# The w_out stage of a fused attention and MoE kernel as seven products of quarters per batch, with one set of eight PSUM places

## The chip, the cores and the metric

The kernel runs on one core of a Trainium2 chip. The metric is the time of one execution on the device in microseconds. The median of three runs before the change is 670.9 us, the lowest 670.52 and the highest 672.65.

## The reference

Three blocks follow one another: attention over 4 batches, a first MoE block, and a second one, which alone is changed. With `x` the output of the first block (4 batches of 576 tokens and 512 features):

```python
def _moe2_ref(x, w_in, g_ln, w_sg, b_sg, w_out):
    h = x @ w_in                                   # 512 -> 1024
    h = gelu_tanh(h)
    u, v = (h[..., :512], h[..., 512:])
    v_n = (v - mean(v)) / np.sqrt(var(v) + 1e-06) * g_ln
    v_s = np.einsum('ts,bsd->btd', w_sg, v_n) + b_sg[None, :, None]
    gated = u * v_s
    return (x + gated @ w_out).astype(np.float32)  # w_out: 512 x 512
```

## The kernel before

All work is recorded first and emitted later, so nearly every instruction has the line of the emitter (L664) in the profile; one tells them apart by the names of their tiles. Each large product is made three times over: both operands are kept as a high part (type fp32r) and a low rest, and high times high, high times low and low times high are added up in PSUM (`passes`, L872). Making such a pair costs a copy on ScalarE (`copy`) and a subtraction on VectorE or GpSimd (`sub`); the table `WHO` (L667) says on which engine.

The second MoE block runs batch by batch (b = 0 to 3), each with these stages:

- **V** (`stage_v`, L1608): x times the second half of w_in, token tiles of 128 as rows, 12 matmuls of 512 columns per tile, into PSUM tiles `V`; then gelu on ScalarE, the normalisation on VectorE (`st`, `ag`, `rs`, `vt`), and the pair `vh`, `vl`. Even batches have a fifth tile for the last 64 tokens of two batches.
- **U** (`stage_u`, L1667): x times the first half of w_in, 8 groups of 12 matmuls of 288 columns, into PSUM tiles `M`, then gelu into `U`.
- **S** (`stage_s`, L1682): w_sg times the normalised v, 8 groups of 14 matmuls of 288 columns, into `M`. Behind each group VectorE scales it into `gt`, GpSimd multiplies by `U`, ScalarE copies to `gh`, VectorE subtracts to `gl`.
- **O** (`stage_o`, L1723): w_out times the gated values, for two batches at once: 3 column blocks of 384 by 4 row blocks, each a group of 12 matmuls of 384 columns into PSUM tiles `O`. One VectorE instruction (two where a block spans both batches) adds half of `X2` and writes `o`, which SyncE stores.

The order of the recorded stages is V0 U0 S0, V1 U1 S1, V2 O(0,1) U2 S2, V3 U3 S3, O(2,3). PSUM has three rings of places in this block: 3 for `V`, 3 for `M`, 2 for `O`. `w_out` is loaded as 64-bit words and turned to single precision by five VectorE and two ScalarE instructions of 1024 columns for each half (`w_bits`, `w_pair`), among the work of S0. A list scheduler (`Plan.schedule`) then plays the recorded instructions through a table of durations and fixes each engine's order; within one ring, places are given out in the recorded order.

Of the kernel before, what the change touches and what calls it, by code (L numbers as in the profile page):

```python
# [11 lines left out]
I32 = mybir.dt.int32  # L12
# [314 lines left out]
class Plan:  # L327
# [337 lines left out]


WHO = dict(oN="A", wl="V", wc="V", Q="A", K="A", Ql="P", Kl="P", V="A", Vl="P", PH="A", O="A", xh="A", xl="P", kh="A", kl="P",  # L667
           X="A", Xl="V", vh="V", vl="V", gU="P", gh="A", gl="V", sg="A", sl="V", R2="AV", R="A", P="VA", PL="V", um="A")
ALT = 400.0
MB = 100  # L670
CB = 300
# [35 lines left out]
LD1 = 6  # L707
AHEAD = 3
T1 = 2


def cost(n):
    return n / 2.4 + 13
# [3 lines left out]
def fused_kernel(ctx: ExitStack, tc: tile.TileContext, low, high, tails, mu,  # L717
# [114 lines left out]
    def w_bits(key, vtile):  # L832

        raw = w1[key]
        low, high = raw[:, :, :, 0], raw[:, :, :, 1]
# [735 lines left out]
    def wt3(shape, dt):  # L1571
        return gtile(shape, dt, "w", 2)

    def ut3():
        return gtile([128, 1024], I32, "u", 1).rearrange("p (c n) -> p c n", n=512)

    loads, conv = weight_list(("wout", w_out, 4, (0,), 1.0, wt3, ut3))
# [30 lines left out]
    def stage_v(b):  # L1608
# [73 lines left out]
    def stage_s(b):  # L1682
        vh, vl = VN.pop(b)
        vt = VT.pop(b)
        sh, sl = sg
        if b % 2 == 0:
            GT[b // 2] = gtile([128, 4, 2 * S], F32R, "gh"), gtile([128, 4, 2 * S], F32R, "gl")
        gh, gl = [x[:, :, S * (b % 2):S * (b % 2) + S] for x in GT[b // 2]]
        order.need(("V", b), ("U", b))
        for f in range(2):  # L1690
            fs = slice(f * HF, (f + 1) * HF)
            for m in range(4):
                ms = slice(128 * m, 128 * m + 128)
                p, mk = ptile("M", HF, 3)
                pe(14 * cost(HF))
                for c in range(4):
                    mm(p, vh[:, c, ms], sh[:, c, fs], start=c == 0)
                    mm(p, vh[:, c, ms], sl[:, c, fs])
                    mm(p, vl[:, c, ms], sh[:, c, fs])
                mm(p, vt[:, ms], sh[:, 4, fs])  # L1700
                mm(p, vt[:, ms], sl[:, 4, fs], stop=True)
                gt = gtile([128, HF], F32, "gt", 2)

                def e0(p=p, gt=gt, m=m, fs=fs):
                    nc.vector.scalar_tensor_tensor(out=gt, in0=p, scalar=g_col[:, m:m + 1], in1=b_bc[:, fs],
                                                   op0=ALU.mult, op1=ALU.add)

                def e1(gt=gt, m=m, fs=fs):
                    tt("gU", gt, gt, U[b][:, m, fs], ALU.mult)

                def e2(gt=gt, m=m, fs=fs):
                    copy("gh", gh[:, m, fs], gt)

                def e3(gt=gt, m=m, fs=fs):
                    sub("gl", gl[:, m, fs], gt, gh[:, m, fs].bitcast(F32))

                at(0, e0, mk)
                at(400, e1)
                at(1200, e2)
                at(1700, e3, ("G", b, f))  # L1720
                yield

    def stage_o(p2):  # L1723
        gh, gl = GT.pop(p2)
        W = 2 * S // 3
        for f in range(3):
            fs = slice(W * f, W * f + W)
            spans = [(2 * p2 + x, max(W * f, S * x), min(W * f + W, S * x + S)) for x in range(2) if W * f < S * x + S and S * x < W * f + W]
            order.need(*[("G", b, g) for b, t0, t1 in spans for g in range(2)])
            for m in range(4):  # L1730
# [3 lines left out]
                o = gtile([128, W], F32, "o", 3)  # L1734

                def e0(p=p, o=o, m=m, spans=spans, f=f):
                    for b, t0, t1 in spans:
                        os, xs = slice(t0 - W * f, t1 - W * f), slice(t0 - S * (b % 2), t1 - S * (b % 2))
                        nc.vector.scalar_tensor_tensor(out=o[:, os], in0=X2[b][:, m, xs], scalar=0.5, in1=p[:, os], op0=ALU.mult, op1=ALU.add)
                        nc.sync.dma_start(out=outT[b, 128 * m:128 * m + 128, xs], in_=o[:, os])  # L1740

                at(0, e0, mk)
                yield

    load_tails(0)
    load_x2(0)
    take(loads, 99)
# [3 lines left out]
    raw4, raw1 = gtile([128, 4, 2 * S], F32, "gh")[:, :, 0:S], gtile([128, 4, 2 * S], F32, "gl")[:, 0, 0:S]  # L1751
# [9 lines left out]
    work += conv  # L1761
    for b in range(B):
        for _ in stage_v(b):
            pass
        if b == 2:
            for _ in stage_o(0):
                pass
        for _ in stage_u(b):
            take(work)
        if b + 1 < B:  # L1770
# [3 lines left out]
            XHL[b + 1] = wtile([128, 2, 4, S], F32R, "XHL")  # L1774
            for t in range(5):
                at(1000 + 1500 * t, lambda t=t, b=b: split_x2(b + 1, 128 * t, min(S, 128 * t + 128)), ("xs", b + 1, t))
        for _ in stage_s(b):
            take(work)
    for _ in stage_o(1):
        pass  # L1780
    order.run()
    plan.schedule()
    plan.emit()
    for p in (pcm, gcm, wcm, dram, const):
        p.close()


# [62 lines left out]
```

## Time and profile before

| what | value |
|---|---|
| median of three runs | 670.9 us |
| the profiled execution | 669.56 us, of which 667.5 us are the span of the profile |
| granted TensorE clock over the span | 0.999 |
| TensorE matmuls busy | 659.0 us (99%), 4074 of them |
| VectorE busy | 471.4 us (71%) |
| ScalarE busy | 420.2 us (63%) |
| GpSimd busy | 231.8 us (35%) |
| second MoE block on TensorE | from 453.4 to 664.1 us |

The page gives busy time of each engine, the same in 40 slices, and the chain of work that ended last. The views of the trace used below are the chain in order of time, groups of instructions by form in a stretch, the instructions of one tile, busy time by stretch, and the order of time on one engine. A matmul's listed duration is longer than the distance to the next one, since they are pipelined; the distance is read from the chain.

### The profile page before, as it was taken

What the parts mean: (1) busy time and instruction counts of PE and PEld (TensorE: products, weight loads), DVE (VectorE), ACT (ScalarE), POOL (GpSimd) and SP (SyncE); (2) the same over time, 40 slices, a digit from 0 to 9 for tenths busy, and PEclk for the clock granted to TensorE, in tenths of its full rate; (3) what the DMA queues carried; (4) which work ended last, traced back from release to release, by engine and by line L of the source; (5) the groups of instructions that cost most, each with busy time, mean ns of one, the idle gap of its engine ahead of it and who ended that gap; (6) DMA issues with size and microseconds to landing.
All of it is one profiled execution on the core that took longest, in us unless ns stands there. A gap on an engine that the chain in (4) does not pass through costs nothing.

```text
span 667.5 us, 11918 instructions
## 1 busy us (share of the span) xinstructions
PE 659.0 (99%) x4074; PEld 608.9 (91%) x4074; DVE 471.4 (71%) x1306; ACT 420.2 (63%) x1095; POOL 231.8 (35%) x278
## 2 busy tenths in 40 slices
PE   9999999999999999999999999999999999999997
PEld 8978777889999999999999889998999989998997
DVE  4979999997678888886886766765796574166232
ACT  6998987689867999898888865834433320132210
POOL 3033334146613456565454513601151410041220
PEclk9999999999999999999999999999999999999999
DMA  9894421233224345321233008207700002300012
GB/s 333 308 357 149 162 93 36 99 120 105 67 76 125 98 141 163 114 59 58 98 122 105 26 2 299 72 25 225 275 2 1 1 0 88 127 1 1 1 50 92
DMA packets 35244, 71.36 MB, mean 107 GB/s; under 512 B 6256, under 2 KB 18032, under 8 KB 35184
## 3 DMA queue, kind: packets, MB, share of 16 engines
q1 hardware_dynamic: 35040, 70.60, 31.4%
q8 instruction: 32, 0.52, 0.4%
q14 instruction: 28, 0.23, 0.1%
q10 hardware_dynamic: 144, 0.00, 0.0%
HBM read 59.05 MB, written 9.44 MB: 103 GB/s over the span
## 4 chain that ended last, share of the span: by engine, by line
PE 82%; ACT 7%; DVE 5%; DMA 3%; issue 2%; SPq 1%; POOL 0%; ACTq 0%; DVEq 0%; POOLq 0%
PE M L664 40%; PE O L664 18%; PE S L664 10%; PE T L664 8%; PE V L664 6%; ACT P L664 2%; DMA w<-w_out_dram 1%; DVE wv L664 1%; DMA q<-Q 1%; ACT wv L664 1%; DVE P L664 1%; DVE PL L664 1%; DVE xT L664 1%; SPq L664 1%; DMA kh<-low_dram 0%
## 5 line engine op out<-in xcount | busy, mean ns | idle before, releaser
L664 ACT ACTIVATE PH<-T 128x384 fp32r<-128x384 f32 (+3 forms) x152 | 65.8, 434 | 31.5 <-PE T L664 27.3
L664 DVE TENSOR_TENSOR PL<-T,PH 128x384 fp32r<-128x384 f32 (+1 forms) x128 | 63.4, 504 | 31.4 <-ACT PH L664 20.5
L664 PE MATMUL M<-xh,w 128*128 128x384 f32 (+1 forms) x272 | 75.8, 341 | 0.0
L664 PE MATMUL M<-xh,wv 128*128 128x256 f32 (+2 forms) x264 | 71.6, 359 | 0.0
L664 PE MATMUL M<-kh,wv 128*128 128x320 f32 (+2 forms) x256 | 70.1, 347 | 0.0
L664 PE MATMUL T<-ident,P 128*128 128x128 f32 x320 | 68.7, 277 | 1.3 <-DVE PL L664 0.5
L664 ACT ACTIVATE P<-S,nb 128x128 f32<-128x128 f32 (+2 forms) x124 | 65.7, 538 | 6.4 <-DVE P L664 5.6
L664 DVE TENSOR_SCALAR_CACHE_REDUCE P<-S 128x128 f32<-128x128 f32 (+2 forms) x124 | 58.7, 489 | 15.0 <-PE S L664 8.6
L664 POOL TENSOR_TENSOR gt<-gt,U 128x288 f32<-128x288 f32 x32 | 30.9, 968 | 95.9 <-ACT XHL L664 48.6
L664 POOL TENSOR_TENSOR Q<-qkv,Q 64x256 fp32r<-64x256 f32 x32 | 25.2, 787 | 108.9 <-ACT Q L664 79.6
L664 POOL TENSOR_TENSOR xl<-t,xh 128x384 fp32r<-128x384 f32 (+1 forms) x40 | 39.8, 1002 | 49.6 <-ACT xh L664 47.1
L664 PEld LDWEIGHTS T<-ident,P 128*128 128x128 f32 x320 | 42.2, 141 | 13.6 <-DVE P L664 3.7
L664 POOL TENSOR_TENSOR kl<-R,kh 128x384 fp32r<-128x384 f32 (+1 forms) x40 | 41.1, 1031 | 37.0 <-ACT kh L664 36.9
L664 PE MATMUL M<-XHL,w 128*128 128x288 f32 x384 | 51.7, 294 | 0.0
L664 PEld LDWEIGHTS M<-XHL,w 128*128 128x128 f32 x384 | 51.4, 188 | 0.2
L664 PE MATMUL O<-gh,w 128*128 128x384 f32 x192 | 49.6, 337 | 0.0
L664 PEld LDWEIGHTS M<-xh,w 128*128 128x128 f32 x272 | 48.1, 189 | 1.4
L664 PEld LDWEIGHTS M<-xh,wv 128*128 128x128 f32 x264 | 46.8, 189 | 2.5
L664 ACT ACTIVATE U<-M 128x288 f32<-128x288 f32 x32 | 12.9, 410 | 57.5 <-PE M L664 57.5
L664 PE MATMUL M<-kl,wv 128*128 128x256 f32 (+2 forms) x160 | 48.3, 349 | 0.0
L664 POOL TENSOR_TENSOR V<-qkv,V 128x320 fp32r<-128x320 f32 (+1 forms) x48 | 34.9, 737 | 38.4 <-ACT V L664 33.1
L664 PEld LDWEIGHTS M<-kh,wv 128*128 128x128 f32 x256 | 45.2, 189 | 1.9
(216 smaller groups left out, 1895.5 us busy)
## 6 DMA issues: line engine op xcount, KB each, us to landing
qkv<-high_dram SPq DMA_DIRECT2D x32, 544.0 KB, 4.7
qkv<-low_dram SPq DMA_DIRECT2D x22, 320.0 KB, 3.4
tail<-tails_dram SPq DMA_DIRECT2D x16, 352.0 KB, 3.2
X<-x2d SPq DMA_DIRECT2D x4, 1152.0 KB, 11.1
w<-w_k_dram SPq DMA_DIRECT2D x4, 1024.0 KB, 10.7
w<-w_v_dram SPq DMA_DIRECT2D x4, 1024.0 KB, 5.1
w<-w_in_dram SPq DMA_DIRECT2D x4, 1024.0 KB, 8.4
outT_dram<-o SPq DMA_DIRECT2D x16, 192.0 KB, 1.9
```

The source lines that it names most:

```text
L664: getattr(getattr(self.nc, e), fn)(*pos, **{k: real(x) for k, x in a.items() if k[0] != "_"})
```

## The change

The w_out product of each batch is made by one level of Strassen's scheme. w_out's 512 by 512 matrix is cut into four quarters (`a11` to `a22`, 256 by 256), and the gated values of a batch (512 features by 576 tokens) into four quarters `b11` to `b22` of 256 by 288. Eight products of quarters become seven, of sums and differences:

- Weights: four extra sums or differences on VectorE (`wT`, written in place over the unpacked words `u`), and seven pairs `wo` of 512 columns (ScalarE copy, VectorE subtraction) in the place of two of 1024.
- Gated values: for each batch and each half j of the features (a half is two row blocks of 128, j and j + 2), four differences `t1` to `t4` (`T`, VectorE or GpSimd), and seven pairs of 288 columns (in `g`, ScalarE copy and VectorE subtraction) in the place of four.
- `stage_o` now takes one batch: 2 output halves by 7 products, each a group of 6 matmuls of 288 columns. Behind the products of each half stand eleven additions and scalings of 288 columns (VectorE, one of them VectorE or GpSimd) and one ScalarE copy.
- The recorded order becomes V0 U0 S0, V1 O0 U1 S1, V2 O1 U2 S2, V3 U3 S3, O2 O3.
- PSUM of this block is one ring `B` of eight places for all stages.
- For room in SBUF, `X2` has 2 buffers for 3, `U` 1 for 2, the gated pair is one tile `g` per batch (the last batch's in a pool of its own that opens when the w_in weights are done with), and the raw words of w_out and w_sg land in what is later the first `g`. The loads of w_out are issued ahead of those of w_sg.

```diff
+GT_BUFS = 8
+O_BUFS = 4
+ORDER_O = (1, 6, 2, 5, 7, 4, 3)
...
+    def bank(w):
+        t, key = ptile("B", 512, 8)
+        return t[:, 0:w], key
...
-        X2[b] = gtile([128, 4, S], F32, "X2", 3)
+        X2[b] = gtile([128, 4, S], F32, "X2", 2)
...
-            p, mk = ptile("V", 512, 3)
+            p, mk = bank(512)
...
-        U[b] = gtile([128, 4, S], F32, "U", 2)
+        U[b] = gtile([128, 4, S], F32, "U")
...
-                p, mk = ptile("M", HF, 3)
+                p, mk = bank(HF)
...
+        GT[b] = (gtile if b < B - 1 else etile)([128, 2, 7, 2, HF], F32R, "g")
...
+                def both(n, x):
+                    copy("gh", g[:, 0, n, j, :], x)
+                    sub("gl", g[:, 1, n, j, :], x, g[:, 0, n, j, :].bitcast(F32))
+
+                both(0, b11)
+                sub("T", t3, b22, b12)
+                both(6, t3)
+                sub("T", t1, b12, b11)
+                both(4, t1)
+                both(1, b21)
+                sub("T", t2, b22, t1)
+                both(5, t2)
+                sub("T", t4, b21, t2)
+                both(3, t4)
+                both(2, b22)
...
-            for m in range(4):
-                p, mk = ptile("O", W, 2)
-                pe(12 * cost(W))
-                passes(p, "wout", 4, m, gh[:, :, fs], gl[:, :, fs])
...
+            def product(n, j=j, ps_of=ps_of):
+                p, k = ps_of[n] = bank(HF)
+                pe(6 * cost(HF))
+                for c in range(2):
+                    wh, wl = [WO[:, i, n - 1, c, 128 * j:128 * j + 128] for i in range(2)]
+                    mm(p, wh, g[:, 0, n - 1, c, :], start=c == 0)
+                    mm(p, wh, g[:, 1, n - 1, c, :])
+                    mm(p, wl, g[:, 0, n - 1, c, :], stop=c == 1)
...
+                if n == 1:
+                    copy("p1", u, p)
+                    half_x("11", p)
+                if n == 2:
+                    add(o["11"], p, o["11"])
+                    store("11")
+                if n == 6:
+                    add(u, p, u)
+                if n == 5:
+                    add(w, p, u)
+                    half_x("12", w)
+                if n == 7:
+                    half_x("22", p)
+                    add(o["22"], o["22"], w, "oadd")
+                    store("22")
+                    add(u, p, u)
+                    half_x("21", u)
+                if n == 4:
+                    add(o["21"], p, o["21"])
+                    store("21")
+                if n == 3:
+                    add(o["12"], p, o["12"])
+                    store("12")
...
+    for f in (lambda: wout_bits(0), lambda: wout_bits(1),
+              lambda: (wout_pair(0, a11), wout_pair(1, a12)),
+              lambda: (wout_pair(3, a22), wout_tt(a22, a21, a22, ALU.add), wout_pair(4, a22)),
+              lambda: (wout_tt(a21, a11, a21, ALU.subtract), wout_pair(6, a21)),
+              lambda: (wout_tt(a11, a22, a11, ALU.subtract), wout_pair(5, a11)),
+              lambda: (wout_tt(a12, a12, a11, ALU.subtract), wout_pair(2, a12))):
+        work.append(plan.rank(CB, f))
...
-        if b == 2:
-            for _ in stage_o(0):
+        if b in (1, 2):
+            for _ in stage_o(b - 1):
```

Up to the second MoE block the engines' orders are the same but for two neighbouring ScalarE instructions. Three places show what moved in it.

TensorE, from V of batch 1 on, before. `V<-w,XHL` is the V stage, `M<-XHL,w` the U stage, `M<-sgh,vh` and its like the S stage.

```order
L664 MATMUL V<-w,XHL 128x512 x48
L664 MATMUL M<-XHL,w 128x288 x96
L664 MATMUL M<-sgh,vh 128x288
L664 MATMUL M<-sgl,vh 128x288
L664 MATMUL M<-sgh,vl 128x288
```

The same place in the changed kernel, where `B` is any PSUM place and `B<-g,wo` a product of the O stage:

```order
L664 MATMUL B<-w,XHL 128x512 x48
L664 MATMUL B<-g,wo 128x288 x84
L664 MATMUL B<-XHL,w 128x288 x96
L664 MATMUL B<-sgh,vh 128x288
L664 MATMUL B<-sgl,vh 128x288
```

The O stage of batch 0 (84 matmuls) now stands between V and U of batch 1. Before, the first O stage stood behind V of batch 2.

VectorE at that place, before: the end of S of batch 0 (`gl`), the last steps of w_out (`u`, `w`) and the normalisation of V of batch 1 (`st`, `ag`, `rs`, `vt`; `vh` and `vl` follow).

```order
L664 SCALAR_TENSOR_TENSOR u<-w,u 128x1024
L664 BN_STATS st<-vt 128x6
L664 TENSOR_TENSOR gl<-gt,gh 128x288
L664 BN_AGGR ag<-st 128x2
L664 TENSOR_TENSOR w<-u,w 128x2x512
L664 TENSOR_SCALAR rs<-ag 128x1
L664 BN_STATS st<-vt 128x6
L664 BN_AGGR ag<-st 128x2
L664 TENSOR_SCALAR vt<-vt,ag,rs 128x512
```

In the changed kernel (`u<-u` is a sum or difference of weight quarters, `wo` a low part of the seven weight pairs, `g` a low part of the gated pairs, `o` and `uw` the additions behind the products):

```order
L664 TENSOR_TENSOR g<-gt,g 128x288
L664 BN_STATS st<-vt 128x6
L664 TENSOR_TENSOR u<-u 128x2x256
L664 TENSOR_TENSOR wo<-u,wo 128x512
L664 TENSOR_TENSOR u<-u 128x2x256
L664 TENSOR_SCALAR vt<-vt,ag,rs 128x512
L664 TENSOR_TENSOR wo<-u,wo 128x512 x2
L664 TENSOR_TENSOR u<-u 128x2x256
L664 CAST vh<-vt 128x512
L664 TENSOR_TENSOR g<-gt,g 128x288
L664 TENSOR_TENSOR vl<-vt,vh 128x512
L664 TENSOR_TENSOR wo<-u,wo 128x512
```

The last `wo` row is the last part of the weights; the additions behind the O products of batch 0 come right after it, and most of the normalisation of batch 1 between and after them.

VectorE from the last scalings of S of batch 3 (`gt<-M`), before (`X_5585` and `X_6671` are the inputs of batches 2 and 3):

```order
L664 SCALAR_TENSOR_TENSOR gt<-M,g_col,b_bc 128x288
L664 TENSOR_TENSOR gl<-gt,gh 128x288 x2
L664 SCALAR_TENSOR_TENSOR o<-X_5585,O 128x384 x4
L664 SCALAR_TENSOR_TENSOR o<-X_5585,O 128x192
L664 SCALAR_TENSOR_TENSOR o<-X_6671,O 128x192
```

In the changed kernel from the same scaling on (`X_6318` is the input of batch 2, `gt<-gt` a difference of gated quarters):

```order
L664 SCALAR_TENSOR_TENSOR gt<-B,g_col,b_bc 128x288
L664 TENSOR_TENSOR g<-gt,g 128x288
L664 SCALAR_TENSOR_TENSOR o<-X_6318,B 128x288
L664 TENSOR_TENSOR uw<-B,uw 128x288
L664 TENSOR_TENSOR gt<-gt 128x288
L664 TENSOR_TENSOR g<-gt,g 128x288
L664 TENSOR_TENSOR o<-B,o 128x288
L664 TENSOR_TENSOR uw<-B,uw 128x288
L664 TENSOR_TENSOR g<-gt,g 128x288
L664 TENSOR_TENSOR gt<-gt 128x288
L664 TENSOR_TENSOR g<-gt,g 128x288 x2
```

Before, 18 VectorE instructions follow that scaling up to the end of the kernel. Now 52 do: 6 low parts and 2 differences of the gated values of batch 3, among the first of the 44 additions and scalings of the O stages of batches 2 and 3.

## Rows read from the trace of the kernel before

**Rows 1.** The page: busy us of the engines, share of the span, instructions.

```profile
PE 659.0 (99%) x4074; PEld 608.9 (91%) x4074; DVE 471.4 (71%) x1306; ACT 420.2 (63%) x1095; POOL 231.8 (35%) x278
```

**Rows 2.** Chain that ended last: start us, length us, engine, PSUM tile, instructions.

```profile
480.34 15.11 PE M L664 x112
...
506.33 27.55 PE M L664 x208
...
638.87 25.29 PE O L664 x144
```

**Rows 3.** Groups by form, 480 to 667.5: count, busy us, mean ns, idle before.

```profile
L664 PE MATMUL O<-gh,w 128*128 128x384 f32 x192 | 49.6, 337 | 0.0
...
L664 PE MATMUL O<-gl,w 128*128 128x384 f32 x96 | 32.4, 337 | 0.0
...
L664 DVE TENSOR_TENSOR gl<-gt,gh 128x288 fp32r<-128x288 f32 x32 | 19.0, 593 | 6.3 <-ACT gh L664 6.0
...
L664 DVE BATCH_NORM_STATS2 st<-vt 128x6 f32<-128x512 f32 x13 | 9.0, 691 | 2.4 <-ACT vt L664 2.4
L664 DVE SCALAR_TENSOR_TENSOR o<-X,O 128x384 f32<-128x384 f32 x16 | 8.8, 553 | 18.1 <-PE O L664 15.8 <-DMA outT_dram<-o 2.3
...
L664 DVE TENSOR_TENSOR vl<-vt,vh 128x512 fp32r<-128x512 f32 x12 | 8.3, 689 | 0.1
...
L664 DVE TENSOR_SCALAR vt<-vt,ag,rs 128x512 f32<-128x512 f32 x13 | 7.0, 541 | 6.0 <-POOL rs L664 6.0
...
L664 DVE CAST vh<-vt 128x512 fp32r<-128x512 f32 x12 | 5.1, 422 | 0.1
L664 DVE SCALAR_TENSOR_TENSOR o<-X,O 128x192 f32<-128x192 f32 x16 | 5.0, 351 | 12.0 <-PE O L664 12.0
...
L664 DVE TENSOR_TENSOR w<-u,w 128x1024 fp32r<-128x1024 f32 x2 | 2.4, 1219 | 0.1
L664 DVE BATCH_NORM_AGGREGATE ag<-st 128x2 f32<-128x6 f32 x13 | 2.3, 176 | 0.1
...
L664 DVE TENSOR_SCALAR rs<-ag 128x1 f32<-128x1 f32 x13 | 1.9, 149 | 0.1
```

**Rows 4.** VectorE in order of time: start us, us, instruction, [idle before <-releaser].

```profile
458.33 0.69 DVE L664 BATCH_NORM_STATS2 st<-vt 128x6 f32<-128x512 f32 x1 [4.13 <-ACT vt L664]
...
480.02 1.42 DVE L664 TENSOR_SCALAR u<-u 128x1024 f32<-128x1024 f32 x2 [3.00 <-ACT u L664]
...
493.17 0.52 DVE L664 SCALAR_TENSOR_TENSOR gt<-M,g_col,b_bc 128x288 f32<-128x288 f32 x1
493.60 0.68 DVE L664 TENSOR_SCALAR u<-u 128x1024 f32<-128x1024 f32 x1
...
510.38 0.55 DVE L664 TENSOR_SCALAR vt<-vt,ag,rs 128x512 f32<-128x512 f32 x1 [0.44 <-POOL rs L664]
...
511.43 0.69 DVE L664 TENSOR_TENSOR vl<-vt,vh 128x512 fp32r<-128x512 f32 x1
```

**Rows 5.** ScalarE in order of time, its first copy of w_sg.

```profile
462.94 2.41 ACT L664 ACTIVATE sgh<-gh 128x576 fp32r<-128x576 f32 x4 [0.54 <-DMA gh<-w_sgT_dram]
```

**Rows 6.** Instructions on gt, 480 to 500: duration ns min/median/max, first and last start.

```profile
L664 POOL TENSOR_TENSOR gt<-gt,U x8: 851/1008/1650, 485.1 to 497.4; 128x288 f32<-128x288 f32 x8
...
L664 DVE TENSOR_TENSOR gl<-gt,gh x7: 443/759/1059, 486.8 to 498.3; 128x288 fp32r<-128x288 f32 x7
```

**Rows 7.** Busy us by stretch: length, PE, PEld, DVE, ACT, POOL, clock, DMA.

```profile
506.30:533.90 27.60, 27.60 (x210) 27.60 (x209) 15.20 (x32) 9.21 (x21) 8.55 (x9) 1.00 0.01 1
```

**Rows 8.** The end in order of time, TensorE and VectorE.

```profile
663.81 0.33 PE L664 MATMUL O<-gh,w 128*128 128x384 f32 x1
664.18 0.56 DVE L664 SCALAR_TENSOR_TENSOR o<-X,O 128x384 f32<-128x384 f32 x1 [1.55 <-PE O L664]
```

**Rows 9.** Busy us by stretch at the end; the seventh column is the granted clock.

```profile
665.60:666.10 0.50, 0.00 (x0) 0.00 (x0) 0.00 (x0) 0.00 (x0) 0.00 (x0) 1.00 0.95 350
...
666.60:667.10 0.50, 0.00 (x0) 0.00 (x0) 0.00 (x0) 0.00 (x0) 0.00 (x0) 0.50 0.00 0
```

More of the change, by code (lines that the diff above doesn't have):

```diff
@@ L834, in w_bits @@
         raw = w1[key]
-        low, high = raw[:, :, :, 0], raw[:, :, :, 1]
+        low, high = [raw[(slice(None),) * (len(raw.shape) - 1) + (i,)] for i in range(2)]
         u = vtile()
@@ L1723, in stage_o, with e0, e1, e2 @@
[L1723 to L1730, printed above, removed]
-                p, mk = ptile("O", W, 2)
-                pe(12 * cost(W))
-                passes(p, "wout", 4, m, gh[:, :, fs], gl[:, :, fs])
[L1734 to L1742, printed above, removed]
+        for j in range(2):
+            gts = {}
+            for f in range(2):
+                fs = slice(f * HF, (f + 1) * HF)
+                for k in range(2):
+                    m = j + 2 * k
+                    ms = slice(128 * m, 128 * m + 128)
+                    p, mk = bank(HF)
+                    pe(14 * cost(HF))
+                    for c in range(4):
+                        mm(p, vh[:, c, ms], sh[:, c, fs], start=c == 0)
+                        mm(p, vh[:, c, ms], sl[:, c, fs])
+                        mm(p, vl[:, c, ms], sh[:, c, fs])
+                    mm(p, vt[:, ms], sh[:, 4, fs])
+                    mm(p, vt[:, ms], sl[:, 4, fs], stop=True)
+                    gt = gts[k, f] = gtile([128, HF], F32, "gt", GT_BUFS)
+                    def e0(p=p, gt=gt, m=m, fs=fs):
+                        nc.vector.scalar_tensor_tensor(out=gt, in0=p, scalar=g_col[:, m:m + 1], in1=b_bc[:, fs],
+                                                       op0=ALU.mult, op1=ALU.add)
+                    def e1(gt=gt, m=m, fs=fs):
+                        tt("gU", gt, gt, U[b][:, m, fs], ALU.mult)
+                    at(0, e0, mk)
+                    at(400, e1)
+                    yield
+            def e2(gts=gts, j=j):
+                b11, b12, b21, b22 = gts[0, 0], gts[0, 1], gts[1, 0], gts[1, 1]
+                t1, t2, t3, t4 = [gtile([128, HF], F32, "gt", GT_BUFS) for _ in range(4)]
+                g = GT[b]
+                def both(n, x):
[12 more added lines that the diff above has]
+                both(2, b22)
+            at(1400, e2, ("G", b, j))
@@ new lines, in stage_o, with half_x, add, store @@
+    def stage_o(b):
+        g = GT.pop(b)
+        order.need(("G", b, 0), ("G", b, 1))
+        for j in range(2):
+            o = {k: gtile([128, HF], F32, "o", O_BUFS) for k in ("11", "12", "22", "21")}
+            u, w = [gtile([128, HF], F32, "uw", 2) for _ in range(2)]
+            ps_of = {}
+            def product(n, j=j, ps_of=ps_of):
[6 more added lines that the diff above has]
+                    mm(p, wl, g[:, 0, n - 1, c, :], stop=c == 1)
+            def half_x(k, x, j=j, o=o):
+                i, f = int(k[0]) - 1, int(k[1]) - 1
+                nc.vector.scalar_tensor_tensor(out=o[k], in0=X2[b][:, j + 2 * i, HF * f:HF * f + HF], scalar=0.5, in1=x,
+                                               op0=ALU.mult, op1=ALU.add)
+            def add(out, x, y, who="ps"):
+                tt(who, out, x, y, ALU.add)
+            def store(k, j=j, o=o):
+                m, f = j + 2 * int(k[0]) - 2, int(k[1]) - 1
+                nc.sync.dma_start(out=outT[b, 128 * m:128 * m + 128, HF * f:HF * f + HF], in_=o[k])
+            def after(n, ps_of=ps_of, o=o, u=u, w=w, half_x=half_x, add=add, store=store):
+                p = ps_of[n][0]
+                if n == 1:
[21 more added lines that the diff above has]
+                    store("12")
+            for n in ORDER_O:
+                product(n)
+                at(0, lambda n=n, after=after: after(n), ps_of[n][1])
@@ L1746, in fused_kernel @@
     load_x2(0)
-    take(loads, 99)
+    flat = gtile([128, 14 * S], F32, "g")
+    wout = [flat[:, 2048 * c:2048 * c + 2048].bitcast(I32) for c in range(2)]
+    for c in range(2):
+        nc.sync.dma_start(out=wout[c].rearrange("p (c n) -> p c n", n=1024),
+                          in_=w_out[256 * c:256 * c + 256, :].rearrange("(c p) n -> p c n", p=128))
     nc.sync.dma_start(out=g_col, in_=g_ln)
@@ L1760, in fused_kernel, with wout_bits, wout_pair, wout_tt @@
         work.append(sgs)
-    work += conv
+    WO = gtile([128, 2, 7, 2, 256], F32R, "wo")
+    wv = [gtile([128, 1024], I32, "u", 2) for _ in range(2)]
+    def wout_bits(c):
+        w1["wout", c] = wout[c].rearrange("p (n two) -> p n two", two=2)
+        w_bits(("wout", c), lambda: wv[c])
+    def wout_pair(n, x):
+        hi, lo = [WO[:, i, n] for i in range(2)]
+        copy("wo", hi, x)
+        sub("wol", lo, x, hi.bitcast(F32))
+    (a11, a21), (a12, a22) = [[x[:, :, 256 * i:256 * i + 256] for i in range(2)] for c in range(2)
+                              for x in [wv[c].bitcast(F32).rearrange("p (c n) -> p c n", n=512)]]
+    def wout_tt(out, a, b, op):
+        tt("wT", out, a, b, op)
+    for f in (lambda: wout_bits(0), lambda: wout_bits(1),
[5 more added lines that the diff above has]
+        work.append(plan.rank(CB, f))
     for b in range(B):
@@ L1776, in fused_kernel @@
                 at(1000 + 1500 * t, lambda t=t, b=b: split_x2(b + 1, 128 * t, min(S, 128 * t + 128)), ("xs", b + 1, t))
+        if b == B - 1:
+            ecm, etile = pool("moe2g", side="right", after=[wcm])
         for _ in stage_s(b):
             take(work)
-    for _ in stage_o(1):
-        pass
+    for b in (2, 3):
+        for _ in stage_o(b):
+            pass
     order.run()
@@ L1783, in fused_kernel @@
     plan.emit()
-    for p in (pcm, gcm, wcm, dram, const):
+    for p in (pcm, gcm, ecm, dram, const):
         p.close()
```

39 lines of the change are left out of this document (3 added, 36 removed).

## Prediction

> **What bounds the kernel now.** I read the page's busy times first: TensorE works 659.0 of 667.5 us [rows 1], so time is won by giving it less work and lost wherever another engine makes it wait. The chain of waits in order of time says the same of the second MoE block: from 480.34 us to the last matmul it is matmuls alone, stage after stage [rows 2]. Then come the groups by form [rows 3], for the price of each kind of instruction, and VectorE in order of time [rows 4], since the change takes work from TensorE and gives work to VectorE. A difference is worked out against the profiled execution's 669.56 us and then set on the median, 670.9, which lies 1.3 us above it. A measurement of this kernel can tell about 0.3% from no change, here 2.0 us.
>
> **TensorE: 6.1 us less.** The last O stage is 144 matmuls of 384 columns in 25.29 us, 0.1756 us each; U and S of batch 1 are 208 matmuls of 288 columns in 27.55 us, 0.1325 each [rows 2]. Before, O has 192 + 96 matmuls [rows 3]: 288 x 0.1756 = 50.6 us. After, 4 batches x 2 halves x 7 products x 6 matmuls = 336, all of 288 columns: 336 x 0.1325 = 44.5 us. Nothing else on TensorE changes in number or shape. In the 288-column stages the weight loads are busy 27.60 of 27.60 us [rows 7], so a matmul there may already be paced by its load; that is inside the 0.1325.
>
> The Trainium skill (TensorE: Matmul & The Clock Gate, section "Wait — 56ns, not 53.3ns?") gives N / 2.4 GHz plus 2.5 ns from one matmul to the next; by that the saving would be 46.8 - 41.2 = 5.6 us, an estimate from that page. The rows show 12 ns over N / 2.4 GHz at 288 columns and 16 at 384, so here the rows decide.
>
> **The head of the block: nothing.** The two w_out loads (1024 KB each) now stand ahead of w_sg's 1440 KB on SyncE's queue. Before, w_sg was there by 462.94 [rows 5], 9.5 us after the block began (453.4), and is first needed by S of batch 0 at 480.34 [rows 2]. At the same pace 2048 KB more cost at most 13.5 us: 476.5. The cover is 17.4 us, so this costs 4 us less than would show. The gain there is VectorE's: it idles 3.00 us for w_out's unpacking before 480.02 [rows 4], and this goes.
>
> **The O stage of batch 0: +1.8 us.** Here is the tight place. Before, w_out had until V of batch 2; now its seven pairs must be ready between V and U of batch 1, and on VectorE they stand behind S of batch 0. TensorE would be through V of batch 1 at 506.33 [rows 2]. A product takes 6 x 0.1325 = 0.795 us; in the changed order the one of the last weight pair (number 3) is seventh, so its weights are due at 506.33 + 6 x 0.795 = 511.1. The seven products of the other half are queued on TensorE behind it.
>
> When does VectorE deliver? Before, from 458.33 to the end of V's normalisation of batch 1 at 511.43 + 0.69 = 512.12, it took 53.8 us; less the 3.00 for w_out, 50.8 [rows 4]. Up to the last weight part the changed queue holds the same work, less what now comes later or is gone: two low parts of 1.22 (2.4), the normalisation of 2 tiles (0.691 + 0.176 + 0.149 + 0.541 + 0.422 + 0.689 = 2.67 each) and of a third without its first step (1.98), one 512-column subtraction (0.69) and the last 256 columns of XHL (0.4): 10.8 us [rows 3]. New are 7 low parts and 4 sums of 512 columns, at vl's 0.689 for a subtraction of that shape: 7.6 us; and 6 low parts and 5 differences of 288 columns [rows 3]. Their price is the uncertain one: gl takes 0.443 undisturbed, 0.593 in the mean, 0.759 as the median of S of batch 0 while GpSimd works on the same tiles [rows 3, 6]. Eleven of them are 4.9, 6.5 or 8.4 us. So the last weight part is there at 458.33 + 50.8 - 10.8 + 7.6 + 4.9 = 510.8, or 512.4, or 514.3: TensorE waits 0, 1.3 or 3.2 us. I take the mean price, since GpSimd now has 11 operations there (8 multiplications and 3 differences) for 8, and add 0.5 for one more wait of the sort that VectorE has for GpSimd (0.44) [rows 4]: 1.8 us. A wait here is lost for good, as TensorE has no idle time left to make it up.
>
> **The later O stages: nothing.** The O stage of batch 1 follows V of batch 2, whose 60 matmuls of 512 columns give VectorE 13.6 us between S and O, at the pace of the 48 that V of batch 1 runs in 10.9 (from 480.34 + 15.11 to 506.33 [rows 2]), and there are no weights to make. U of the next batch reuses places that O's additions must have read: eleven instructions per seven products are 11 x 0.45 = 5.0 us against 7 x 0.795 = 5.6 on TensorE, and eight places let it run seven products ahead. X2 with two buffers and U with one are refilled a stage or more before they are read. SyncE stores 32 pieces as before.
>
> **The end: +1.1 us.** O of batches 2 and 3 is 168 matmuls, 22.3 us after the last S. Behind the last scaling of S VectorE has 52 instructions. Between 0.351 at 192 columns and 0.553 at 384, an addition of 288 columns out of PSUM takes 0.45 [rows 3]; 44 of them are 19.9 us, the 8 on the gated values at 0.593 are 4.7, the scaling before them 0.52: 25.1. It can end no sooner than one addition behind the last matmul, 22.3 + 0.45 = 22.7. By durations VectorE is thus 2.4 us late; but an instruction that waits for nothing is followed before it ends (493.17 to 493.60 for one of 0.52 [rows 4]), and 0.09 less for each of 52 makes 20.4, no lateness at all. Half of the additions wait for the one before, so I take the middle, 1.2. The last addition takes 0.45 for the 0.56 of today [rows 8]: -0.1. VectorE's queue before, one addition per group, had idle time here throughout.
>
> **Sum.** -6.1 + 1.8 + 1.1 = -3.2 us: the profiled execution at 666.4, the median at **667.7 us**. The bounds: no wait at all, -6.2 or 664.7; the upper prices at both places and a second half microsecond, -6.1 + 3.7 + 2.3 = -0.1 or 670.8.
>
> **The rivals.**
>
> *VectorE covers its work* (0.12): its queue overlaps as in its best stretches and both waits vanish: 664.7. For it: VectorE is busy 71% of the span [rows 1], and 3.00 us of idle time before S of batch 0 are freed. Against it: the median of 0.759 in just that stretch.
>
> *The gain is eaten, no change to be told* (0.17): both places at or above their upper price, some 670. For it speaks that VectorE's new instructions mostly have two inputs in SBUF and stand in a stretch that is dense already.
>
> *VectorE becomes the bound of S and O of batch 0: slower* (0.10). While GpSimd multiplies and subtracts, low parts reach 1.059 us and GpSimd's own operations 1.650 for 0.851 [rows 6]: one holds up the other. If all 19 low parts and differences there took 1.059, the 11 new ones would be 11.6 us instead of 6.5 and the 8 old ones 3.7 us more than they hold in the 50.8: the last weight part at 512.4 + 0.5 + 8.8 = 521.7, a wait of 10.6; if half of them did, 6.2. The turning point is 5.0 us of waiting at product 3 (6.1 less the end's 1.1), weights at 516.1. And such a pause costs twice: at the end of the span the granted clock is still full at 665.6 to 666.1 and at its lower level (0.50, 1.2 GHz) from 666.6, some 2.5 us after TensorE stopped [rows 9], so the products after a pause of that length may run at half speed. Between the two, with 8.4 us of waiting: -6.1 + 8.4 + 1.1 = +3.4, and 674.3.
>
> The Trainium skill (SBUF — State Buffer, section "Who interferes with whom") says that a VectorE instruction with two SBUF inputs contends with a GpSimd instruction that reads SBUF, by an exclusive lock where the loser blocks in full. By that rule this rival would be the likely one. The rows agree on the sort of instruction but not on the rate: in the mean of 32 a low part loses only 0.15 us [rows 3].
>
> *The matmuls do not get cheaper* (0.02): if groups of 6 cost per matmul what O's groups cost, 0.1756, 336 are 59.0 us, 8.4 more: some 682. Groups of 12 and 14 at 288 columns both run at 0.1325, which speaks against it.
>
> **How the numbers follow.** The forecast proper, between 665 and 668.9, has 0.59. Faster by over 0.3% (below 668.9) is that and the first rival: 0.71. Within 0.3%: 0.17. Slower: the last two, 0.12. The range from 664.8 to 670.7 leaves out most of the two slower cases and about half of the first rival.
>
> **What would show it.** Right: 336 matmuls of 288 columns in O at 0.132 to 0.133 us apart; TensorE's idle time in this block in one place, before or within O of batch 0, put down to VectorE's or ScalarE's `wo`, 0 to 4 us; none before U or S; VectorE dense over the last 25 us, with its last addition 0.5 to 3 us behind the last matmul. Wrong: waits of TensorE for PSUM places before U, for `g` before an O stage of batches 1 to 3, or for w_sg in S of batch 0; a granted clock below 0.99 in the block; low parts of a mean above 0.8 us.

## The result, and the profile after

The changed kernel takes **664.5 us** (median, 662.7 to 665.4) where the kernel before takes 670.9: 0.9896 of it, with a 95% interval of 0.987 to 0.992. That is 6.4 us, or 1%, faster. The forecast was 3.2 us faster, 667.7, and the time lies 0.3 us under the range. It is the first rival that came out, VectorE covering its work (664.7). One execution in a later run of the changed kernel took 2811.6 us, for a reason that stays open, and neither its time nor its trace is used here.

The profiled execution took 665.41 us. Its page, against [rows 1]; columns are busy us, share of the span, instructions:

```profile
span 663.3 us, 12181 instructions
PE 653.3 (98%) x4122; PEld 602.6 (91%) x4122; DVE 520.4 (78%) x1413; ACT 433.8 (65%) x1132; POOL 247.8 (37%) x292
```

TensorE has lost 5.7 us of busy time with 48 more instructions, and VectorE has gained 49 us with 107 more. The chain of waits in order of time (start us, length us, what), against [rows 2]:

```profile
455.73 201.37 PE B L664 x1364
...
657.86 0.81 DVE o L664 x2
...
658.96 0.87 DVE o L664 x3
```

One piece of 201 us is TensorE alone: it waits for nothing in the second MoE block, from V of batch 0 to within 3 us of its last matmul. Only then does VectorE stand in the chain. The groups by form, 480 to 663.3 us, against [rows 3] (count, busy us, mean ns, idle before):

```profile
L664 PE MATMUL B<-g,wo 128*128 128x288 f32 x336 | 45.0, 295 | 0.0
...
L664 DVE TENSOR_TENSOR g<-gt,g 128x288 fp32r<-128x288 f32 x56 | 35.4, 657 | 2.1 <-ACT g L664 2.0
L664 POOL TENSOR_TENSOR gt<-gt,U 128x288 f32<-128x288 f32 x32 | 31.4, 990 | 65.1 <-DVE gt L664 38.2 <-ACT XHL L664 25.1 <-ACT g L664 1.8
L664 DVE TENSOR_TENSOR gt<-gt 128x288 f32<-128x288 f32 x21 | 10.9, 536 | 2.3 <-POOL gt L664 2.3
...
L664 DVE TENSOR_TENSOR wo<-u,wo 128x512 fp32r<-128x512 f32 x7 | 4.6, 683 | 0.0
```

The 336 matmuls are there, with no idle time before any of them. The block is best measured by itself, from the start of the first matmul of V of batch 0 to the end of the last matmul. Its start before (its end is in [rows 8]):

```profile
453.45 11.05 PE L664 MATMUL V<-w,XHL 128*128 128x512 f32 x48
```

Its start and its end after:

```profile
455.57 11.05 PE L664 MATMUL B<-w,XHL 128*128 128x512 f32 x48
...
654.79 4.96 PE L664 MATMUL B<-g,wo 128*128 128x288 f32 x36
```

It runs from 453.45 to 664.14 before and from 455.57 to 659.75 after. These are 210.69 and **204.18 us, 6.51 less**. What lies behind the last matmul, the tail, grew from 3.36 to 3.55 (spans are given to 0.1 us, so a tail is good to 0.05). So the trace accounts for 6.3 us, and the times for 6.4. That the profiled executions themselves differ by 4.2 us only comes from the part ahead of the block, which lasted 2.1 us longer in the one of after; it is the same work in both, in the same order but for two neighbouring ScalarE instructions, and its length varies (last section).

The tight place, O of batch 0, on TensorE in order of time (start us, length us, instruction):

```profile
507.74 11.27 PE L664 MATMUL B<-g,wo 128*128 128x288 f32 x84
518.84 5.45 PE L664 MATMUL B<-XHL,w 128*128 128x288 f32 x40
```

84 matmuls in 11.10 us, 0.1321 each, without a gap. VectorE around the last weight part (the same columns):

```profile
510.48 0.42 DVE L664 CAST vh<-vt 128x512 fp32r<-128x512 f32 x1
510.81 0.45 DVE L664 TENSOR_TENSOR g<-gt,g 128x288 fp32r<-128x288 f32 x1
511.18 0.68 DVE L664 TENSOR_TENSOR vl<-vt,vh 128x512 fp32r<-128x512 f32 x1
511.78 0.68 DVE L664 TENSOR_TENSOR wo<-u,wo 128x512 fp32r<-128x512 f32 x1
512.39 0.45 DVE L664 SCALAR_TENSOR_TENSOR o<-X,B 128x288 f32<-128x288 f32 x1
512.75 0.45 DVE L664 TENSOR_TENSOR uw<-B,uw 128x288 f32<-128x288 f32 x1
```

The last `wo` ended at 512.46. The first matmul that needs this low part is the 39th of O: 507.74 + 38 x 0.1325 = 512.78. The part is that matmul's weights, and they are loaded just before it:

```profile
512.64 0.19 PEld L664 LDWEIGHTS B<-g,wo 128*128 128x128 f32 x1
```

VectorE was **0.2 us early**. One reason is in the same rows: an instruction of 0.68 is followed after 0.60, one of 0.45 after 0.36.

The end, against [rows 8], VectorE in order of time, with the idle time before:

```profile
655.43 0.46 DVE L664 SCALAR_TENSOR_TENSOR o<-X,B 128x288 f32<-128x288 f32 x1 [0.42 <-ACT uw L664]
...
657.12 0.46 DVE L664 TENSOR_TENSOR uw<-B,uw 128x288 f32<-128x288 f32 x1 [0.87 <-PE B L664]
...
659.69 0.81 DVE L664 TENSOR_TENSOR o<-B,o 128x288 f32<-128x288 f32 x2
```

VectorE waits for TensorE here, so it has caught up. It ends at 660.50, 0.75 behind the last matmul, against 0.60 before.

### The profile page after: what moved, and what is told of

It is laid out like the page before. It is cut to its first block, busy times and chain, and to the rows that moved or that the text cites. A ratio compares the mean times of both kernels' runs of the same rounds, so it can differ in the third digit from the quotient of the medians.

```text
span 663.3 us, 12181 instructions
## 1 busy us (share of the span) xinstructions
PE 653.3 (98%) x4122; PEld 602.6 (91%) x4122; DVE 520.4 (78%) x1413; ACT 433.8 (65%) x1132; POOL 247.8 (37%) x292
## 4 chain that ended last, share of the span: by engine, by line
PE 83%; ACT 7%; DVE 4%; DMA 3%; issue 1%; POOL 1%; DVEq 0%; ACTq 0%; SPq 0%; POOLq 0%
PE B L664 30%; PE M L664 25%; PE S L664 10%; PE O L664 10%; PE T L664 8%; ACT P L664 2%; DMA qkv<-high_dram 2%; DMA q<-Q 1%; ACT wv L664 1%; DVE wv L664 1%; ACT PH L664 1%; DVE P L664 1%; DVE PL L664 1%; DVE xT L664 0%; DMA kh<-low_dram 0%
## 5 line engine op out<-in xcount | busy, mean ns | idle before, releaser
L664 POOL TENSOR_TENSOR kl<-R,kh 128x384 fp32r<-128x384 f32 (+1 forms) x40 | 43.3, 1088 | 35.9 <-ACT kh L664 35.8
L664 ACT ACTIVATE g<-gt 128x288 fp32r<-128x288 f32 x56 | 23.4, 442 | 45.6 <-POOL gt L664 34.1
L664 PE MATMUL B<-XHL,w 128*128 128x288 f32 x384 | 51.5, 294 | 0.0
L664 PEld LDWEIGHTS B<-XHL,w 128*128 128x128 f32 x384 | 51.2, 188 | 0.2
L664 PE MATMUL O<-PH,V 128*128 128x320 f32 (+3 forms) x192 | 46.6, 302 | 1.4 <-ACT PH L664 1.3
```

What stands on the lines that cost most here:

```text
L664: getattr(getattr(self.nc, e), fn)(*pos, **{k: real(x) for k, x in a.items() if k[0] != "_"})
```

## The experiments

Theory A: the gain is TensorE's time alone, and VectorE's new work hides since it costs its start-to-start time, 0.60 us per 512 columns and 0.37 per 288. Theory B: VectorE costs its listed durations and is nearly the bound. A third possibility was that the PSUM set made part of the gain. "Block" and "tail" are measured as above; the start is that of the block. Each ratio is to the kernel before as measured beside that run, so two rows can differ a little otherwise by time than by ratio. For the changed kernel's second time there are times alone.

```
kernel                           start    block   tail   time    of before (95%)
before (first trace)             453.45  210.69   3.36   670.9
before, second trace             456.51  210.76   3.33   670.7   0.9998 (0.9982-1.0013)
changed                          455.57  204.18   3.55   664.5   0.9896 (0.9869-0.9924)
changed, second time                                     663.7   0.9892 (0.9876-0.9909)
changed, third time              454.98  204.18   3.54   663.8   0.9897 (0.9874-0.9919)
before, one PSUM set             455.21  210.41   3.38   669.7   0.9975 (0.9964-0.9985)
the same again                   454.73  210.41   3.36   670.4   0.9989 (0.9974-1.0004)
changed, sets of 3, 3, 2         456.61  208.33   3.26   668.8   0.9964 (0.9951-0.9977)
changed, sets of 2, 3, 3         454.79  204.90   3.51   665.0   0.9912 (0.9887-0.9937)
weights' low parts twice         455.27  208.26   3.57   668.5   0.9952 (0.9940-0.9965)
weights' low parts four times    454.73  215.59   3.58   676.0   1.0079 (1.0052-1.0106)
more additions at the end        455.56  204.17   7.47   668.0   0.9962 (0.9947-0.9976)
six products                     456.13  197.84   4.03   658.6   0.9817 (0.9797-0.9836)
differences all on VectorE       455.82  204.18   3.50   664.9   0.9915 (0.9900-0.9930)
```

**The two kernels again.** The changed kernel a second and a third time:

> The changed kernel again, beside the kernel before, to fix the size of the gain and to have a trace of the same chip for the runs beside it. Theory A (TensorE's time alone: 288 x 0.1756 - 336 x 0.1325 = 6.1 us, VectorE's new work all hidden): 0.991 of before, 664.5 to 665, and the second MoE block (first V matmul of batch 0 to the last matmul) 6 to 6.6 us shorter than before in the trace. Theory B (VectorE's listed durations, as forecast): 0.995, 667.7, with a wait of 1 to 3 us before product 3 in O of batch 0.

> The changed kernel once more, for a second trace of its own: the block 204.2 us again, no wait of TensorE in it, and the time 0.989 to 0.991 of before. If VectorE had been ready for product 3 by luck alone (some 1 us of slack), a wait of up to 1 us shows here in O of batch 0.

The gain repeats (0.989 to 0.990; the second time's interval lies just under theory A's 0.991), and so does the block in the trace of the third time, to the hundredth: 204.18 us, no wait of TensorE in it. The last `wo` ends there at 511.88; the 39th matmul is due at 507.15 + 38 x 0.1325 = 512.19 and the load of its weights, as in the first trace, 0.13 earlier: a margin of 0.2 us again. It is small, and it repeats, as this part of the program does. And the kernel before:

> The kernel before, unchanged, for a second trace of it: the kernel before with the one PSUM set was 1.7 us faster than the kernel before, while its second MoE block was only 0.28 us shorter in the traces (210.41 to 210.69). Theory A (the block explains the change, the other 1.4 us lie ahead of the block and vary from execution to execution): this trace's block is again 210.7 us, its start lies anywhere from 453 to 457 us, and the time is that of before (0.9985 to 1.0015). Rival (the block itself varies by 1 us or more): a block of 210 or 212 us.

Its block is 210.76, with the start 3.1 us later than in the first trace: theory A.

**The PSUM set alone, in the kernel before.** In each of V, U, S and O:

```diff
-            p, mk = ptile("V", 512, 3)
+            p, mk = bank(512)
...
```

> The kernel before with only the PSUM part of the change: V, U, S and O take their places from one set of eight. Theory A: TensorE waits for PSUM nowhere in this block of the kernel before, bar 0.3 us at the start of S of batch 0, so the time is that of before within 0.5 us (0.9993 to 1.0007). Rival (part of the gain is the PSUM set): 1 to 4 us faster than before.

> The kernel before with the one PSUM set again, for a second trace and time: it was 1.7 us faster than before, of which the block shows 0.3. Theory A (the rest lies ahead of the block, where both programs run the same instructions in the same order, and is not the work of the PSUM set): the block again 210.4 us, and the ratio nearer to 0.9995 than to 0.9975. Rival (the PSUM set does gain 1.4 us somewhere): 0.9975 again.

The block became 0.28 us shorter, both times; the short wait for `U` ahead of S of batch 0 is gone. The first time was 1.7 us under before and thus outside of what theory A gave, the second 0.3 us, within it. Since the instructions ahead of the block are the same in both programs, and in the same order, the block's 0.3 us is what the traces assign to the set. It is the balance of two things: V of batch 1 starts 0.61 us earlier behind the block's start (41.23 us for 41.84), so the wait listed with 0.3 cost twice that from start to start, and the rest of the block takes 0.33 longer. Whether some tenths more come from the part ahead is not settled by these intervals.

**The changed kernel without the PSUM set.** Places as before, three for V, three for U and S, two for O:

```diff
-    def bank(w):
-        t, key = ptile("B", 512, 8)
+    def bank(w, tag="M", n=3):
+        t, key = ptile(tag, 512, n)
...
-            p, mk = bank(512)
+            p, mk = bank(512, "V", 3)
...
-                p, k = ps_of[n] = bank(HF)
+                p, k = ps_of[n] = bank(HF, "O", 2)
```

> The changed kernel with the PSUM places in three sets as before (V 3, U and S 3, O 2), everything else as changed. In O two places let TensorE run only one product ahead of its additions. A product takes 6 x 0.1325 = 0.795 us, the additions after one product take one to four VectorE instructions of 0.37 to 0.45, after product 7 it is four, 1.5 to 1.8 us, and each of these has to come behind what VectorE has queued. Theory A with the single set needed by the seven products: each half of an O stage waits 1 to 2 us, eight halves, 6 to 14 us slower than the changed kernel (1.01 to 1.02 of it), that is, the gain is gone. Rival (the places don't matter): the changed kernel's time within 0.5 us.

The block is 4.15 us longer, 5.1 by the times: most of the gain is lost, though less than expected. TensorE in the last O stage, in order of time:

```profile
653.44 3.48 PE L664 MATMUL O<-g,wo 128*128 128x288 f32 x24 [0.19 <-DVE o L664]
657.08 2.96 PE L664 MATMUL O<-g,wo 128*128 128x288 f32 x18 [0.16 <-DVE o L664]
660.23 3.48 PE L664 MATMUL O<-g,wo 128*128 128x288 f32 x24 [0.19 <-DVE o L664]
```

After each run of matmuls TensorE waits for an addition. What that costs is read from the starts: 653.44 to 657.08 are 3.64 us for 24 matmuls, which take 3.17 at 0.132 each, and 657.08 to 660.23 are 3.15 for 18, which take 2.38. The waits that the profile lists add up to 1.1 us in the whole block, the smaller part of the 4.15. The first two O stages lost next to nothing: V of batch 3 starts 143.37 us behind the block's start, against 143.22 in the changed kernel. There the planner had put matmuls of U and S between the products. The last two have nothing to be put between, and lose about 1 us per half; the expectation charged that to all eight halves. One place more for O, at V's expense:

> The changed kernel with three sets of PSUM places again, but two for V, three for U and S and three for O, instead of 3, 3 and 2, which cost 4.2 us in the block. Theory A (the two places of O are what the seven products lack, one more lets TensorE run a product further ahead): the block comes back to within 1.5 us of the changed kernel's 204.2. Rival (it is the division into sets as such, with V now worse off): a block of 208 us or more.

204.90: 3.4 of the 4.15 us come back. So the seven products need more than two places, and three nearly do. A third place for O is a condition of most of the gain; the one set of eight gives it, and is worth 0.7 us beyond it. Whether those 0.7 are lost because O has three places and not more, or because V has two, was not tried.

**One product less.** `ORDER_O` without its last entry; the output quarter 12 is stored without that product, so this kernel leaves out a part of the result:

```diff
-ORDER_O = (1, 6, 2, 5, 7, 4, 3)
+ORDER_O = (1, 6, 2, 5, 7, 4)
...
                     half_x("12", w)
+                    store("12")
```

> The changed kernel without product 3 of the seven (left out of the computation everywhere, so the output quarter 12 lacks it): 48 fewer matmuls of 288 columns, and 8 fewer additions on VectorE. Theory A (TensorE alone bounds the stages, VectorE is hidden): 48 x 0.1325 = 6.4 us under the changed kernel. Theory B (VectorE is the bound of the O stages already, 10 additions of 0.45 to 6 products of 0.795): 0 to 4 us under.

The block falls by 6.34 us, 48 x 0.132: TensorE's time goes one to one into the block, and VectorE bounds none of the O stages. 0.5 us of it come back in the tail, where VectorE now ends 1.20 behind the last matmul instead of 0.75. By the ratios it is 5.4 us (0.9817 and 0.9897 of before), give or take some 2 us.

**VectorE's margin ahead of product 3.** The seven low parts of `wo`, each made twice, then four times:

```diff
-        sub("wol", lo, x, hi.bitcast(F32))
+        for _ in range(2):
+            sub("wol", lo, x, hi.bitcast(F32))
```

> The changed kernel with each of the seven subtractions that make the low parts of the w_out quarters made twice (same result written twice), 7 more VectorE instructions of 512 columns ahead of O of batch 0. Product 3 was due at 513.2 us and its low part ended at 512.5 in the trace of the changed kernel, 0.8 us of slack. Theory A (in the dense queue an instruction costs its start-to-start time, 0.60 us): the last part comes 4.2 us later, TensorE waits 3.4 us at product 3 of O of batch 0, and the time is 3 to 3.5 us over the changed kernel. Theory B (by the listed 0.68, with no slack left): 4.8 us over. Rival (VectorE has much slack there): nothing.

VectorE, then TensorE in O of batch 0:

```profile
504.79 2.48 DVE L664 TENSOR_TENSOR wo<-u,wo 128x512 fp32r<-128x512 f32 x4
...
516.49 0.69 DVE L664 TENSOR_TENSOR wo<-u,wo 128x512 fp32r<-128x512 f32 x1
```

```profile
511.34 1.06 PE L664 MATMUL B<-g,wo 128*128 128x288 f32 x6 [0.83 <-DVE wo L664]
513.15 1.73 PE L664 MATMUL B<-g,wo 128*128 128x288 f32 x8 [0.74 <-DVE wo L664]
515.35 1.62 PE L664 MATMUL B<-g,wo 128*128 128x288 f32 x8 [0.47 <-ACT wo L664]
517.23 5.55 PE L664 MATMUL B<-g,wo 128*128 128x288 f32 x40 [0.26 <-DVE wo L664]
```

Four of them take 2.48, 3 x 0.60 + 0.69. Counted from the block's start the last part comes 5.0 us later: 7 x 0.60 = 4.2, a wait of 0.46 for ScalarE's high part, and an addition of 0.37 that the planner put ahead. The block is 4.08 longer, between the two theories' 3.5 and 4.8. The difference of 0.9 to the lateness is 0.8 that the planner won back by moving one product of the other half ahead of the late one (the last wait stands before the 45th matmul, no more before the 39th), and 0.1 of margin: the 0.2 of above, less the 0.05 from the end of the part (517.18) to TensorE's start (517.23). The price per instruction is thus theory A's; the margin that I had assumed, 0.8, was too large.

> The changed kernel with each of the seven low-part subtractions of w_out made four times (the same result written four times), 21 more VectorE instructions of 512 columns ahead of the last weight part. Theory A (0.60 us each from start to start, about 1.0 us of slack, as the run with 7 more showed by its 5.0 us of lateness and 4.1 of loss): 12.6 less 1.0, some 11.6 us over the changed kernel, the block at about 215.8. Rival (a pause of TensorE costs twice, since the granted clock falls behind it): 13 us or more over, with a granted clock below 0.99 in O of batch 0.

The block is 11.41 longer, near to theory A's 11.6, but it is made up otherwise. TensorE's idle time in O of batch 0 is 6.3 us; the other 5.1 are matmuls at half clock. Stretches (length, busy us of PE, PEld, DVE, ACT, POOL, granted clock, DMA):

```profile
506.00:511.00 5.00, 1.32 (x7) 0.92 (x5) 5.00 (x9) 0.46 (x1) 0.00 (x0) 0.93 0.00 0
511.00:516.00 5.00, 4.83 (x20) 4.83 (x21) 5.00 (x10) 1.85 (x4) 0.00 (x0) 0.50 0.00 0
516.00:521.00 5.00, 2.53 (x13) 2.06 (x12) 4.97 (x9) 0.63 (x1) 0.00 (x0) 0.84 0.00 0
521.00:526.00 5.00, 5.00 (x27) 4.77 (x28) 4.97 (x11) 0.60 (x1) 0.00 (x0) 0.71 0.10 33
```

Behind a pause of 3.85 us (to 511.17) the granted clock is at its lower level (0.50, 1.2 GHz) for a while, as the third rival had it. That cost nothing extra, since the matmuls at half speed only filled the time until the next weights came. It was back at 0.94 to 1.00 from 517 to 520, and fell a second time behind two shorter waits, 1.46 and 1.01 us, with only four matmuls between them; the 52 matmuls from there on took 8.6 us instead of 6.9, and those 1.7 us did cost. In the run with each part made twice, the waits of 0.26 to 0.83 us left the clock at 1.00. Neither theory is clean here: the rival's clock came, its 13 us did not.

**VectorE's margin at the end.** Each `half_x` addition of batch 3 made three times:

```diff
...
+                for _ in range(3 if b == B - 1 else 1):
...
```

> The changed kernel with the addition of half the input made three times instead of once in the O stage of the last batch (the same result written three times): 16 more VectorE instructions of 288 columns in the last 11 us. Theory A (0.37 us each from start to start, and 1.55 us of VectorE's idle time in this stage to fill): 16 x 0.37 - 1.55 = 4.4 us over the changed kernel, all of it behind the last matmul. Theory B (the listed 0.45 and no slack at the end, as the forecast's upper price had it): 7.2 us over. Rival (VectorE is far from the bound here): under 1 us.

The block is the same to 0.01 us, and the tail is 3.92 us longer. 16 x 0.366 = 5.9 us of work cost 3.9, so VectorE had 1.9 us to spare at the end (theory A gave 1.55). VectorE near the end of this run:

```profile
660.35 0.45 DVE L664 SCALAR_TENSOR_TENSOR o<-X,B 128x288 f32<-128x288 f32 x1
660.72 0.45 DVE L664 SCALAR_TENSOR_TENSOR o<-X,uw 128x288 f32<-128x288 f32 x1
661.08 0.45 DVE L664 TENSOR_TENSOR uw<-B,uw 128x288 f32<-128x288 f32 x1
```

**Differences off GpSimd.**

```diff
-           ... T="VP", ...
+           ... T="V", ...
```

> The changed kernel with all 32 differences of the gated values on VectorE instead of 21 there and 11 on GpSimd. Theory A (VectorE at 0.37 to 0.6 us an instruction with next to no slack ahead of O of batch 0, some 1 us): up to three more differences there, 1.1 to 1.8 us on VectorE, so 0 to 0.9 us over the changed kernel. Theory B (GpSimd's work on the same memory is what slows VectorE's low parts there, from 0.44 to 0.57 in the mean): VectorE gains back what it takes on, and the time is the changed kernel's or up to 1 us under.

The block is again 204.18. The time is 0.9915 of before, where the changed kernel's is 0.9897, with intervals that overlap: no difference. Groups by form of this run, to be set beside those of after:

```profile
L664 POOL TENSOR_TENSOR gt<-gt,U 128x288 f32<-128x288 f32 x32 | 32.6, 1029 | 70.3 <-DVE gt L664 34.5 <-ACT XHL L664 26.2 <-ACT g L664 9.6
L664 DVE TENSOR_TENSOR g<-gt,g 128x288 fp32r<-128x288 f32 x56 | 30.5, 561 | 2.2 <-ACT g L664 2.1
L664 DVE TENSOR_TENSOR gt<-gt 128x288 f32<-128x288 f32 x32 | 16.0, 507 | 2.1 <-POOL gt L664 2.1
```

VectorE took on 11 differences (10.9 to 16.0 us) and got 4.9 us back on its low parts (35.4 to 30.5). Its busy time in the whole program even fell, from 520.4 to 518.2 us, with 11 instructions more:

```profile
PE 653.5 (98%) x4122; PEld 602.8 (91%) x4122; DVE 518.2 (78%) x1424; ACT 433.9 (65%) x1132; POOL 237.9 (36%) x281
```

That is theory B's mechanism, with no time won, as TensorE waits for neither.

No run beats the changed kernel with the whole computation in it. Less work for TensorE is what would, and VectorE has margins of 0.2 us ahead of product 3 and 1.9 at the end to pay for it.

## Why the prediction was wrong, step by step

**TensorE, -6.1: right.** 84 matmuls in 11.10 us, and one product less per half takes 6.34 us off: 0.132 each.

**The head of the block: right.** w_sg's first copy starts 14.4 us behind the block's start, where [rows 5] have 9.5:

```profile
469.94 1.82 ACT L664 ACTIVATE sgh<-g 128x576 fp32r<-128x576 f32 x3
```

S of batch 0 starts at 481.96 and waits for nothing. It was not counted that the wait for `U` before it would go: 0.3 us as listed, 0.6 from start to start. It goes with the PSUM set alone, and it is absent as well from the changed kernel with three sets, so the set is not the only thing that removes it. With the 6.1 of the matmuls it makes 6.7, of which the block shows 6.5.

**O of batch 0, +1.8: this step failed; TensorE waits 0 there.** TensorE's due time was near (57.65 us behind the block's start, measured 57.1 for the load of the weights). VectorE's delivery was forecast at 59.45 (512.4 and the 0.5 for one more wait, less 453.45) and measured at 56.9, 2.6 earlier, even before the lower bound. From the starts of VectorE's instructions in both traces the difference divides about as follows. The eleven 512-column operations took 6.6 instead of 7.6 us, 0.60 each and not 0.689. The 14 low parts of the gated values took 7.2 (0.52 each), where 8 of before (5.6 in that queue) and 6 new at 0.593 made 9.1: the new ones are cheaper than listed, and the old ones too got cheaper. The wait of 0.5 for GpSimd did not come, and its other waits were 0.4 less. Against that, XHL's low parts took 0.6 more, and what I had taken off by listed durations was worth 0.5 less. One error lies in the unit: I added listed durations where the queue runs from start to start. That is some 0.9 of the 2.6 us, an estimate: 1.0 on the 512-column operations and 0.5 on the six new low parts, less the 0.5 that I had taken off too much. The larger part lies in the order: in the new queue the eight low parts of before cost some 0.18 us less each (0.52 for 0.70), and the waits fell away. Why they did is not shown. With the right unit alone the forecast would still have had a wait here, of about 1 us.

**The end, +1.1: this step failed too; it is about +0.2.** Here the unit is all of it. The prediction had the right figure among its bounds (0.09 us less for each of 52 instructions: no lateness) and took the middle, on the argument that half of the additions wait for the one before. In the trace they do not stand back to back: the planner puts another addition between the dependent ones, and the spacing is 0.366 nearly throughout. The last addition ends 0.15 us later behind the last matmul than before, where 1.1 was forecast, and the run with 16 more shows 1.9 us of margin.

**The rivals.** The first was priced to 0.2 us, without the wait for `U`, and given 0.12, against a forecast proper of 0.59; its evidence, that the queue overlaps in its best stretches, was the rule and not the exception. The third rested on the dearest low parts (1.059). They exist here too, up to 1.066, but the median in S of batch 0 is 0.450. The instructions on `gt` and `g` of VectorE in that stretch (ns min/median/max):

```profile
L664 DVE TENSOR_TENSOR g<-gt,g x14: 425/450/1066, 489.6 to 510.8; 128x288 fp32r<-128x288 f32 x14
```

The Trainium skill (Perfetto Trace Analysis, section "Optimizing Scalar/DVE Operations") has the rule that the forecast met in [rows 4] and did not apply here: the latency that a profile lists is longer than the time for which the engine is taken, because its last part overlaps with the next instruction. It gives the engine's own share of the overhead as some 60 ns on SBUF and 125 on PSUM, and the listed latency as about twice that, so the overlapping part would be as long again, an estimate from that page. The trace agrees with the rule, but shows 0.08 us for both: 0.68 listed and 0.60 from start to start for `wo` from SBUF, 0.45 and 0.366 for the additions out of PSUM.

## What to carry to other kernels

Sum a dense queue by the distance from one start to the next, read from a stretch in which that engine waits for nothing; listed durations are right only for the last instruction and for one that something waits for at once. Where a forecast hangs on a margin of a microsecond, 50 instructions at 0.08 us too much each are the whole of it. Price waits in the same way: the matmul behind a wait starts later than the listed idle time says (1.1 us listed, 4.15 lost). When matmul groups get shorter and their results need several operations each, give them more PSUM places: with two, 4.2 of the 6.5 us were lost, and a third gave 3.4 of them back.

## What the runs showed of the hardware that was not expected

GpSimd's 11 differences took nothing off VectorE. Moved to VectorE they cost it 5.1 us, and its 56 low parts, listed at 657 ns in the mean, fell to 561, 4.9 us in all. The Trainium skill (SBUF — State Buffer, section "Who interferes with whom") says that VectorE instructions with two SBUF inputs contend with GpSimd instructions that read SBUF. The traces agree in so far as the low parts got shorter when the differences left GpSimd. The price would be some 0.45 us per GpSimd instruction, spread over many of VectorE's: an estimate, 4.9 us over 11, from two kernels whose orders also differ elsewhere.

The part of the program ahead of the second MoE block took between 453.45 and 456.61 us in the 13 traces, with the same instructions in the same order (but for those two of ScalarE), while the block repeats to 0.1 us in the three kernels that have two traces. TensorE's waits for DMA in that part, as far as the list of waits shows them, run from 0.7 to 3.0 us, and they do not follow its length: 0.7 in the trace whose block starts at 455.21, 2.9 in the one that starts at 454.79. What decides the length was not tried. A difference of 2 us between two single profiled executions therefore says nothing of a change in the block, and the block's own length does.
